# Three transfers for each block of weights, with the first half issued ahead of the store of a converted piece

## The chip, the core and the metric

The kernel runs on one NeuronCore of a Trainium2 chip. The metric is the device time of one execution in microseconds (us), as the median of several runs. The engines are named as in the profile: PE multiplies matrices, ACT (ScalarE), DVE (VectorE) and POOL (GpSimd) work on tiles, and SP issues the transfers between the chip's main memory (DRAM) and the on-chip memory. PE writes its products to the accumulation memory (PSUM), from which ACT and DVE take them.

## What is computed

Attention over a window of 128 keys feeds a mixture of eight experts, and its output feeds a dense two-layer block. Cut to what matters:

```python
def reference(**kwargs):
    attn_out = _attn_ref(q, k, v)                       # 4 x 8 x 576 x 64
    x = attn_out.transpose(0, 2, 1, 3).reshape(2304, 512)
    # mixture of experts: P is softmax(x @ w_gate), normalised 8 times over rows and columns
    for e in range(8):
        h = np.maximum(x @ w1[e], 0.0)                  # 512 -> 1024
        out += P[:, e:e + 1] * (h @ w2[e])              # 1024 -> 512
    # dense block
    h = out @ w_in                                      # 512 -> 2048
    return (np.maximum(0.01 * h, h) @ w_out).astype(np.float32)
```

All inputs are float32 but `w_in` and `w_out` of the dense block, which are float64: 512 x 2048 and 2048 x 512 numbers. [...]

## The kernel before

**Chunks.** The hidden dimension is cut into chunks of 512: 16 chunks of the experts (two for each) and 4 of the dense block, 20 in all. For each chunk the kernel needs a 512 x 512 block of the first weight (`W[0]`) and one of the second (`W[1]`). The tokens are cut into 18 tiles of 128, taken in five pairs of groups (`PAIRS`). For each chunk and pair `a_steps` makes the hidden values (matmuls at L732) and `b_steps` multiplies them by the second weight (matmuls at L849) and adds the result to `acc`. Both use a Strassen-like scheme of seven products of half blocks, and each factor is split into a high and a low float16 part. `merge` interleaves the steps of the one with those of the other.

**A block of weights** (class `Weights`). `load` brings it from DRAM into `raws[0]` or `raws[1]`, tiles of 128 partitions by 4 slots by 512 float32; a slot is 256 KB. There is one such tile for each of the two weights, and it is used again for every chunk. Then `largest` (L580, ACT) squares each of the four slots and sums the squares; `scale_jobs` makes a power of two from the sums (DVE at L413, a small PE matmul at L421, then more DVE work, and a second small matmul at L440); `scaled` (L583, ACT) multiplies each slot by it; `sums` (L607, POOL) and `part` (L446 on ACT, L447 on POOL) make the seven float16 factors.

**A float64 piece** (`to_single`). There are 32 pieces of 128 x 512 numbers. `load` (L655) brings one as 1024 words a partition, which fill slots 0 and 1 of the same raw tile; slot 2 (`fac`) takes sign and exponent, slot 3 (`man`) the mantissa. Five jobs follow: `exponent` (L661 on DVE, L664 on ACT), `signed` (L667, DVE), `high` (L672 on DVE, L673 on ACT), `low` (L679 on ACT, then POOL's addition at L681, the last reader of the words in slots 0 and 1), and `put` (POOL's multiplication at L685 of slot 2 with slot 3 into slot 3, and the store of slot 3 to DRAM at L686). The stored pieces are the weights of the last four chunks.

**Who uses which tile.** `side_jobs` lists the side work of a chunk: up to three pieces, the loads of the next chunk's weights (`a` into `raws[0]`, `b` into `raws[1]`), and their scaling. The first piece lies in `raws[0]`, and `a.load` comes after its `put`; the second and third piece lie in `raws[1]`, and `b.load` comes after the `put` of the third. Ten chunks convert three pieces each, an eleventh two; there `b.load` doesn't follow a third piece.

**Order.** `tick` takes a job from the list after most steps of the matmuls and holds its instructions on ACT, DVE and POOL behind the latest evictions (`anchor`); transfers are not held so. Within these limits and those of the data, a scheduler fixes the order of instructions on each engine at build time, after a simulated timeline (`schedule_with_timeline_sim=True` at the end of the file). On the chip each engine runs its instructions in that order and stands where one has to wait. All transfers are issued by SP, in its order. A transfer into a slot has to wait until the last reader or writer of that slot is done.

In the load before, the first transfer covers slots 0 to 2 and so waits for the multiplication (it reads slot 2); the second covers slot 3 and waits for the store to land.

Of the kernel before, what the change touches and what calls it, by code (L numbers as in the profile page):

```python
# [31 lines left out]
def attn_moe_kernel(  # L32
# [12 lines left out]
    nc = tc.nc  # L45
    P = 128
# [5 lines left out]
    KT = DM // P  # L52
# [496 lines left out]
    chunks = []  # L549
# [14 lines left out]
    class Weights:  # L564
# [5 lines left out]
            self.mx = small.tile([P, 4], F32, tag="mxw", name="mxw")  # L570

        def load(self):
            self.raw = raws[self.which]
            src = chunks[self.ci][self.which].rearrange("(k p) f -> p k f", p=P)
            for ks in (slice(0, KT - 1), slice(KT - 1, KT)):
                nc.sync.dma_start(self.raw[:, ks], src[:, ks])

        def largest(self, k):
            junk = stg.tile([P, FC], BF16, tag="junk", bufs=1, name="junk")
# [55 lines left out]
    def weights(ci):  # L635
        for which in range(2):
            W[which][ci] = Weights(ci, which)

    def to_single(n, place):
# [48 lines left out]
        def words_f32(w):  # L688
            return w.bitcast(F32)

        return load, [exponent, signed, high, low, put]


# [307 lines left out]

    cast = list(range(2 * KT * (F2 // FC)))

    def side_jobs(ci, n):

        todo = [to_single(cast.pop(0), place) for place in range(min(n, len(cast)))]
        weights(ci)
        a, b = W[0][ci], W[1][ci]
        jobs = [load for load, _ in todo[:2]]
        if not todo:  # L1010
            return [a.load, b.load] + [None] * 10 + a.scale() + a.early() + b.scale() + b.early()
        jobs += [None] * 8 + todo[0][1] + [a.load]
        if len(todo) > 1:
            jobs += todo[1][1]
        if len(todo) > 2:
            jobs += [todo[2][0]] + [None] * 4 + a.scale() + todo[2][1] + [b.load] + a.early()
        else:
            jobs += [b.load] + [None] * 8 + a.scale() + a.early()
        return jobs + [None] * 8 + b.scale() + b.early()
# [15 lines left out]
    for n, u in enumerate(units + [None]):  # L1035
        a, b = [], b_steps(*prev)
        if u == LAST:
            held_back = b[7:]
            b = b[:7]
        if u is None:  # L1040
            b = held_back[:3] + [f for two in zip(b, held_back[3:] + [None] * 3) for f in two if f is not None]
        if u is not None:
            ci, p = u
            assert ci < NCE or p in split_pairs
            a = a_steps(ci, p)
            k0 = len(a) - 7
            if p == ends[ci] and ci + 1 < NC:
                a = [[f] + ([lambda j=k - k0: W[0][ci + 1].at(j)] if k >= k0 else []) for k, f in enumerate(a)]
            else:
                a = [[f] for f in a]  # L1050
        if prev[1] == ends[prev[0]] and prev[0] + 1 < NC:
            k0 = len(b) - 7
            b = [[f] + ([lambda j=k - k0: W[1][prev[0] + 1].at(j)] if k >= k0 else []) for k, f in enumerate(b)]
        else:
            b = [[f] for f in b]
        if u is not None and ci >= 1:
            if n and units[n - 1][0] != ci and ci != NCE:
                weigh(ci)
            if p == 4:
                side += side_jobs(ci + 1, 3 if ci < NCE - 1 else 0) if ci + 1 < NC else []  # L1060
# [65 lines left out]
```

## Time and profile before

| | |
|---|---|
| time, median of 3 runs | 1917.11 us (1916.19 to 1918.63) |
| profiled execution: time, span | 1914.87 us, 1913.1 us |
| PE busy | 1848.6 us (97%), 17725 matmuls |
| ACT, DVE, POOL busy | 71%, 69%, 69% |
| loads of expert weights | 32 of 768 KB (median 4.8 us to landing), 32 of 256 KB (3.7 us) |
| loads of float64 pieces | 32 of 512 KB (3.7 and 3.4 us) |
| stores of pieces | 32 of 256 KB (3.3 and 2.2 us) |

The span is the time from the first to the last instruction of the profiled execution, and its own time lies 1.8 us above it. An engine's busy time counts its instructions; where a matmul row is a little longer than its spacing, rows overlap. A row of a timeline gives the start, the duration, the engine, the line in the kernel, the operation, and in brackets how long the engine stood idle before it and what ended that. The attention fills the first 200 us or so, the chunks that convert float64 pieces run from 290 to about 1160 us, then come three loads of expert weights without pieces, and the four chunks of the dense block.

### The profile page before, as it was taken

The page shows a single profiled execution, that of the slowest core. Times are in us where ns is not written, and L with a number is a line of the kernel's source. Part 1 is how long each engine was busy: PE and PEld are TensorE (multiplying, and loading weights), DVE is VectorE, ACT ScalarE, POOL GpSimd, SP SyncE. Part 2 cuts the span into 40 slices and gives each one's busy share as a digit, 9 for nine tenths or more (in the row PEclk, how much of TensorE's full clock was granted, in tenths as well). Part 3 has the DMA queues.
Part 4 walks back from the last instruction along what each step waited for, and adds up shares of the span by engine and source line. Part 5 has one row for each costly group of instructions (what it writes and reads, how often), then busy time and mean ns, then how long its engine had stood idle before and what let it go on. Part 6 is the DMA issues. An engine that isn't in the chain of part 4 may idle for free. (4 is left out here: it accounts for less than half of the span.)

```text
span 1913.1 us, 45183 instructions
## 1 busy us (share of the span) xinstructions
PE 1848.6 (97%) x17725; PEld 1608.6 (84%) x17725; DVE 1317.9 (69%) x3608; ACT 1358.0 (71%) x3123; POOL 1324.6 (69%) x1140
## 2 busy tenths in 40 slices
PE   7899889999999999999999999999999998999999
PEld 5677778888888888988888898988889787889888
DVE  5456567767776777777676767666666687677877
ACT  7978767776767767676776667666675779776754
POOL 3843567777868787876868786685867786666753
PEclk8999999999999999999999999999999999999999
DMA  7522002111111202111121201100001010101002
GB/s 232 172 89 84 2 23 72 46 62 56 40 57 40 84 24 73 53 54 57 40 64 37 79 23 57 45 24 23 24 24 45 1 45 2 36 11 45 2 26 75
DMA packets 61093, 97.80 MB, mean 51 GB/s; under 512 B 4560, under 2 KB 27600, under 8 KB 60880
## 3 DMA queue, kind: packets, MB, share of 16 engines
q1 hardware_dynamic: 60880, 94.93, 15.5%
q8 instruction: 138, 2.26, 0.5%
q14 instruction: 75, 0.61, 0.1%
HBM read 81.81 MB, written 13.11 MB: 50 GB/s over the span
## 5 line engine op out<-in xcount | busy, mean ns | idle before, releaser
L849 PE MATMUL t<-w,h 128*128 128x256 f16 x7560 | 973.3, 273 | 21.8 <-DVE acc L862 10.4
L732 PEld LDWEIGHTS <-w 128*128 128x128 f16 x8400 | 757.2, 98 | 100.3 <-issue 19.2
L849 PEld LDWEIGHTS <-h 128*128 128x128 f16 x7560 | 730.2, 98 | 119.9 <-issue 33.1
L732 PE MATMUL s<-xp,w 128*128 128x256 f16 (+1 forms) x4872 | 610.4, 262 | 10.2 <-ACT q L756 4.5
L862 DVE SCALAR_TENSOR_TENSOR acc<-t,pu,acc 128x256 f32<-128x256 f32 x866 | 407.5, 477 | 203.7 <-PE t L849 158.8
L805 POOL TENSOR_TENSOR h<-s,h 128x1024 f16<-128x1024 f32 x180 | 387.5, 2153 | 132.7 <-ACT h L802 94.6
L732 PE MATMUL sq<-xp,w 128*128 128x256 f16 (+1 forms) x3528 | 448.4, 262 | 3.3 <-DVE s L761 2.9
L860 POOL TENSOR_TENSOR acc<-acc,part 128x256 f32<-128x256 f32 x322 | 234.9, 732 | 270.0 <-ACT part L859 234.9
L447 POOL TENSOR_TENSOR w<-raw,w 128x512 f16<-128x512 f32 x240 | 277.5, 1166 | 43.5 <-ACT w L446 43.3
L761 DVE SCALAR_TENSOR_TENSOR h<-sq,h 128x512 f16<-128x512 f32 (+1 forms) x352 | 192.2, 551 | 75.5 <-ACT h L780 41.4
L859 ACT ACTIVATE part<-t,pu 128x256 f32<-128x256 f32 x322 | 151.6, 471 | 103.5 <-PE t L849 95.5
L802 ACT ACTIVATE h<-s 128x1024 f16<-128x1024 f32 x180 | 189.6, 1053 | 45.6 <-DVE s L761 43.6
L744 ACT ACTIVATE q<-s 128x256 f32<-128x256 f32 x364 | 137.4, 379 | 74.2 <-PE s L732 57.6
L748 DVE SCALAR_TENSOR_TENSOR sq<-sq,q 128x256 f32<-128x256 f32 x352 | 149.2, 425 | 56.1 <-PE sq L732 48.9
L446 ACT ACTIVATE w<-raw 128x512 f16<-128x512 f32 x240 | 147.8, 628 | 7.9 <-PE t L849 5.9
L780 ACT ACTIVATE h<-sq 128x512 f16<-128x512 f32 x176 | 104.2, 592 | 62.4 <-PE t L849 30.7
L761 DVE SCALAR_TENSOR_TENSOR s<-sq,s 128x256 f32<-128x256 f32 x352 | 145.4, 413 | 1.7
L761 DVE SCALAR_TENSOR_TENSOR s<-sq,q 128x256 f32<-128x256 f32 x352 | 131.6, 414 | 16.4 <-ACT q L756 14.3
L748 DVE SCALAR_TENSOR_TENSOR sq<-s,q 128x256 f32<-128x256 f32 x176 | 75.3, 428 | 85.7 <-ACT q L744 80.3
L580 ACT ACTIVATE junk<-raw 128x512 bf16<-128x512 f32 x160 | 100.1, 626 | 29.2 <-DMA raw<-in_moe_w_dram 27.5
L786 ACT ACTIVATE h<-sq 128x256 f16<-128x256 f32 x176 | 66.7, 379 | 74.5 <-DVE sq L748 64.7
L583 ACT ACTIVATE raw<-raw,sr 128x512 f32<-128x512 f32 x160 | 102.4, 715 | 3.4 <-DVE sr L441 2.9
(142 smaller groups left out, 1717.9 us busy)
## 6 DMA issues: line engine op xcount, KB each, us to landing
raw<-in_moe_w_dram SPq DMA_DIRECT2D x32, 768.0 KB, 4.8
k_t<-in_k_dram SPq DMA_DIRECT2D x16, 512.0 KB, 4.0
raw<-in_moe_w_dram SPq DMA_DIRECT2D x32, 256.0 KB, 3.7
raw<-in_moe_w_in_dram SPq DMA_DIRECT2D x16, 512.0 KB, 3.7
raw<-in_moe_w_out_dram SPq DMA_DIRECT2D x16, 512.0 KB, 3.4
q_t<-in_q_dram SPq DMA_DIRECT2D x18, 256.0 KB, 4.3
v_t<-in_v_dram SPq DMA_DIRECT2D x18, 256.0 KB, 2.7
acc<-in_v_dram SPq DMA_DIRECT2D x18, 256.0 KB, 5.8
```

The costliest lines, as they stand in the source:

```text
L446: nc.scalar.activation(out=hi, in_=src, func=AF.Copy)
L447: return nc.gpsimd.tensor_tensor(out=lo, in0=src, in1=hi, op=ALU.subtract)
L732: nc.tensor.matmul(d[b][:, f, :], t[:, wp, kk, ft * P:(ft + 1) * P], XP[p][:, o, kk, xp, :], start=(i == 0 and f == 0 and j in FIRST), sto ...
L744: nc.scalar.activation(out=q[:, k], in_=ps, func=AF.Copy, scale=CS)
L748: nc.vector.scalar_tensor_tensor(out=block(k), in0=ps, scalar=CS, in1=q[:, k], op0=ALU.mult, op1=ALU.add)
L761: nc.vector.scalar_tensor_tensor(out=out, in0=in0, scalar=sc, in1=in1, op0=op0, op1=op)
L802: nc.scalar.activation(out=h[:, 3:7, 0, :], in_=d["s"], func=AF.Copy)
L805: nc.gpsimd.tensor_tensor(out=h[:, 3:7, 1, :], in0=d["s"], in1=h[:, 3:7, 0, :], op=ALU.subtract)
L849: nc.tensor.matmul(ps, h[:, o, hp, f, tt * P:(tt + 1) * P], w[:, wp, ft, :], start=(i == 0 and j in FIRST), stop=(i == 5), skip_group_chec ...
L859: nc.scalar.activation(out=part, in_=ps, func=AF.Copy, scale=s)
L860: nc.gpsimd.tensor_tensor(out=dst, in0=dst, in1=part, op=ALU.add)
L862: nc.vector.scalar_tensor_tensor(out=dst, in0=ps, scalar=s, in1=dst, op0=ALU.mult, op1=ALU.add)
```

## The change

`load` is cut in two. `load_first` brings slots 0 and 1 in one transfer of 512 KB, `load_rest` slots 2 and 3 in a transfer of 256 KB each. Where a load comes right after the `put` of a piece in the same tile, `over` makes `load_first` part of the job of that `put`, ahead of it, and `load_rest` the job after it. The number of jobs in the list stays the same. All other loads call both parts in a row.

```diff
         def load(self):
+            self.load_first()
+            self.load_rest()
+
+        def transfer(self, ks):
+            src = chunks[self.ci][self.which].rearrange("(k p) f -> p k f", p=P)
+            nc.sync.dma_start(self.raw[:, ks], src[:, ks])
+
+        def load_first(self):
             self.raw = raws[self.which]
-            src = chunks[self.ci][self.which].rearrange("(k p) f -> p k f", p=P)
-            for ks in (slice(0, KT - 1), slice(KT - 1, KT)):
-                nc.sync.dma_start(self.raw[:, ks], src[:, ks])
+            self.transfer(slice(0, 2))
+
+        def load_rest(self):
+            for k in range(2, KT):
+                self.transfer(slice(k, k + 1))
...
+    def over(convert, w):
+
+        def ahead():
+            w.load_first()
+            convert[-1]()
+
+        return convert[:-1] + [ahead, w.load_rest]
+
     def side_jobs(ci, n):
...
-        jobs += [None] * 8 + todo[0][1] + [a.load]
+        jobs += [None] * 8 + over(todo[0][1], a)
...
-            jobs += [todo[2][0]] + [None] * 4 + a.scale() + todo[2][1] + [b.load] + a.early()
+            jobs += [todo[2][0]] + [None] * 4 + a.scale() + over(todo[2][1], b) + a.early()
```

## Rows read from the trace of the kernel before

**Rows 1.** Busy time by stretch: stretch, length, engines (instructions), granted clock, DMA share, GB/s.
```profile
290.00:1165.00 875.00, 859.52 (x8172) 759.95 (x8170) 626.91 (x1573) 615.05 (x1334) 666.98 (x559) 1.00 0.17 55
1201.60:1451.20 249.60, 249.60 (x2398) 222.78 (x2397) 162.03 (x434) 162.98 (x360) 175.58 (x151) 1.00 0.08 27
```

**Rows 2.** Waits, whole span: who waited for whom, us in total, times, longest.
```profile
ACT junk L580 <- DMA raw<-in_moe_w_dram: 27.5, 20, 3.9
```

**Rows 3.** Timeline of ACT: first squares after a pause, and one fourth square.
```profile
322.21 0.63 ACT L580 ACTIVATE junk<-raw 128x512 bf16<-128x512 f32 x1 [1.76 <-DMA raw<-in_moe_w_dram]
...
383.87 0.63 ACT L580 ACTIVATE junk<-raw 128x512 bf16<-128x512 f32 x1 [1.27 <-DMA raw<-in_moe_w_dram]
...
555.41 0.63 ACT L580 ACTIVATE junk<-raw 128x512 bf16<-128x512 f32 x1 [1.57 <-DMA raw<-in_moe_w_dram]
...
725.54 0.63 ACT L580 ACTIVATE junk<-raw 128x512 bf16<-128x512 f32 x1 [1.62 <-DMA raw<-in_moe_w_dram]
...
810.46 0.63 ACT L580 ACTIVATE junk<-raw 128x512 bf16<-128x512 f32 x1 [1.19 <-DMA raw<-in_moe_w_dram]
...
896.31 0.63 ACT L580 ACTIVATE junk<-raw 128x512 bf16<-128x512 f32 x1 [2.04 <-DMA raw<-in_moe_w_dram]
...
899.14 0.61 ACT L580 ACTIVATE junk<-raw 128x512 bf16<-128x512 f32 x1
...
1154.80 0.63 ACT L580 ACTIVATE junk<-raw 128x512 bf16<-128x512 f32 x1 [1.16 <-DMA raw<-in_moe_w_dram]
```

**Rows 4.** Timeline of ACT: exponent of the first piece, three groups.
```profile
712.79 0.71 ACT L664 ACTIVATE raw<-raw,shift 128x512 int32<-128x512 int32 x1
...
798.14 0.71 ACT L664 ACTIVATE raw<-raw,shift 128x512 int32<-128x512 int32 x1
...
883.13 0.71 ACT L664 ACTIVATE raw<-raw,shift 128x512 int32<-128x512 int32 x1
```

**Rows 5.** Timeline of PE: small matmul of the scale, the same three groups.
```profile
737.84 0.22 PE L421 MATMUL mt<-identb,e 128*1 128x128 bf16 x1
...
822.83 0.22 PE L421 MATMUL mt<-identb,e 128*1 128x128 bf16 x1
...
908.60 0.22 PE L421 MATMUL mt<-identb,e 128*1 128x128 bf16 x1
```

**Rows 6.** Timeline of SP at 890 us: issues; the second row merges two.
```profile
890.47 0.33 SPq L686 DMA_DIRECT2D wout<-raw  x1
890.90 2.10 SPq L576 DMA_DIRECT2D raw<-in_moe_w_dram  x2
```

**Rows 7.** Timeline of POOL at 888 us: addition and multiplication of the first piece.
```profile
887.72 1.37 POOL L681 TENSOR_TENSOR raw<-raw 128x512 f32<-128x512 f32 x1 [1.11 <-ACT raw L673]
889.17 1.28 POOL L685 TENSOR_TENSOR raw<-raw 128x512 f32<-128x512 f32 x1
```

**Rows 8.** DMA issues of 889 to 896.4 us: KB each, us to landing.
```profile
raw<-in_moe_w_dram SPq DMA_DIRECT2D x1, 768.0 KB, 5.4
wout<-raw SPq DMA_DIRECT2D x1, 256.0 KB, 2.2
raw<-in_moe_w_dram SPq DMA_DIRECT2D x1, 256.0 KB, 4.3
```

**Rows 9.** Timeline of PE: first matmuls after idle time, behind pauses of ACT.
```profile
330.08 0.81 PE L732 MATMUL s<-xp,w 128*128 128x256 f16 x6 [0.62 <-ACT q L756]
...
387.76 0.81 PE L849 MATMUL t<-w,h 128*128 128x256 f16 x6 [1.18 <-DVE e L415]
...
560.83 1.47 PE L849 MATMUL t<-w,h 128*128 128x256 f16 x12 [0.42 <-DVE acc L862]
...
1156.11 0.81 PE L732 MATMUL s<-xp,w 128*128 128x256 f16 x6 [0.70 <-ACT q L756]
1157.35 0.81 PE L849 MATMUL t<-w,h 128*128 128x256 f16 x6 [0.42 <-DVE acc L862]
```

**Rows 10.** Timeline of DVE at 387 us: the sum of squares.
```profile
387.16 0.16 DVE L413 TENSOR_REDUCE m<-mxw 128x1 f32<-128x4 f32 x1 [2.95 <-ACT junk L580]
```

## The prediction

> **What bounds the kernel now.** I read the busy time of two stretches first [rows 1]. From 290 to 1165 us, where the float64 weights are converted beside the matmuls, PE is busy 859.52 of 875.00 us: 15.48 us are idle. From 1201.6 to 1451.2, where nothing is left to convert, PE is busy all of 249.60 us. So the matmuls are the bound, and a change of the loads can give back at most the idle time of the stretch that converts (and what the start holds). The granted clock is 1.00 of full speed in both, the upper of the two levels (2.4 GHz), so the clock is no part of the case.
>
> Then the waits [rows 2]: ACT stands 27.5 us in 20 pauses before the squares of L580 (the job `largest`), waiting for a weight that is still on its way. One pause of 3.9 us is in the start; the other 19 (23.6 us together) are in the stretch that converts, about two to a group of weights. [rows 3] shows seven of them: 1.16 to 2.04 us each, always before the first of the four squares.
>
> What a pause is worth is read from PE, not from ACT. From some 630 us on the groups run in the same order, so two marks can be compared between groups: the first exponent of the first piece (L664) [rows 4] and PE's small matmul of the scale (L421) [rows 5], with one pause between them. Group at 798: 822.83 - 798.14 = 24.69 us, pause 1.19. Group at 712: 25.05 us, pause 1.62. Group at 883: 25.47 us, pause 2.04. So from 1.19 to 1.62 the group grows by 0.36 for 0.43 us of pause, and from there by 0.42 for 0.42. **A pause of up to some 1.2 us is covered by PE's backlog; what is beyond costs PE its full length.**
>
> **The change part by part.** *Three transfers for two.* Every load is now 512, 256 and 256 KB instead of 768 and 256. That is one more issue of about 0.33 us on SP per load [rows 6]. In the stretch that converts SP stands most of the time waiting for POOL, so it costs nothing there; what would be late next if the cover were gone is the load of the third piece, which stands behind the last transfer on SP. In the start the two loads stand in a row of other loads; two more issues could hold those back by 0.7 us, against which the first half lands earlier than 768 KB do. I take 0 there, with bounds of +0.7 (the two issues) and -3.9 (the whole pause).
>
> *The first half moves ahead of the multiplication and the store.* It overwrites only the words of the piece (slots 0 and 1), so it waits for POOL's addition (L681), no longer for the multiplication (L685). At 883 the addition ends at 887.72 + 1.37 = 889.09, the multiplication at 889.17 + 1.28 = 890.45 [rows 7]; the 768 KB went out at 890.90 [rows 6]. The first half goes out at about 889.1, 1.8 us earlier. Its 512 KB are not in the trace as a weight load; by the rows beside it, it lands after 2.2 us (256 KB) to 5.4 us (768 KB beside a store) [rows 8]: between 891.3 and 894.5, and I take the middle, 892.9. ACT was ready at 896.31 - 2.04 = 894.27 [rows 3]. So the pause goes, or 0.2 us of it stays. The wait that is added: SP now stands at the first half until the addition is done, with the store behind it; the store itself waits for the multiplication that comes later on the same engine, so nobody is held up by that.
>
> *Third quarter.* It still waits for the multiplication and goes out behind the store, where the 768 KB did (890.90). Even with the 4.3 us that 256 KB took behind a large transfer [rows 8] it lands at 895.2; its square is the third, and without the pause two squares of 0.63 us [rows 3] stand before it from 894.27, so it is wanted at 895.5 at the earliest. No cost.
>
> *Last quarter.* It waits for the store to land, as before. Before: out at 890.90 + 2.10 - 0.33 = 892.67 [rows 6], landed 4.3 us later at 896.97 [rows 8], used at 899.14 [rows 3]: 2.17 us to spare, of which the removed pause takes 2.04 in this group and about 1.2 in the usual one. The store now starts with 512 KB in flight ahead of it. If it lands no later, the last quarter is in time, and it no longer shares the engines with 768 KB. If the store takes 4.3 us instead of 2.2 (the row of a 256 KB transfer behind a large one), the last quarter is 2.1 us later: the bounds are 0 and 2.1, and I take under 1, since the first half has a lead of 1.4 us on the store and the last quarter then has the engines to itself. The Trainium skill ("DMA: Bandwidth & Descriptors", section "Queues, rings and completion order") says that each DMA engine takes the descriptors of a ring in their order, by which the store would stand behind what is left of the first half. The 4.3 us of 256 KB behind 768 agree with that; by the rule alone the end at 2.1 would be the nearer one, and it is the third rival below.
>
> *The sum.* Gain where a pause shows on PE. Same-order groups: 0.36 + 0.78 = 1.14 (from the marks above; the pauses near 1.2 count nothing). The other groups differ in order, so I take the idle rows of PE in the wake of a pause [rows 9]. After 383.87: 1.18 us, and here the way is seen: DVE stands 2.95 us at L413 for the last square [rows 10], PE behind DVE. After 555.41: 0.42. After 1154.80: 0.70 + 0.42 = 1.12. After 322.21: 0.62 eight us later, counted half, 0.31. Sum 1.14 + 1.18 + 0.42 + 1.12 + 0.31 = 4.17 us. The profiled execution has a span of 1913.1 and a time of 1914.87 us, 2.2 under the median of the three runs (1917.11); I take the gain off the median: **1917.11 - 4.2 = 1912.9**. Lower bound of the gain: if the cover of 1.2 us holds in the other groups too, only what is beyond it comes back: 0.07 + 0.37 + 0.56 + 1.14 = 2.1 us. Upper bound: 15.48 us, all of PE's idle time in the stretch; half of that is as far as I would go, since PE also idles in groups whose pause is under 1.2.
>
> **The rivals.**
> *The pause only moves, or the cover takes it (no change).* The instructions of ACT and DVE stand in an order that was fixed at build time by a simulated timeline. A pause of about 1 us at nearly every load speaks for squares that were placed where the simulated load had landed. With an earlier first half they may be placed earlier, ahead of evictions, and ACT stands as long as now; or the gaps of PE in [rows 9] are filled with other waits (10 of the 15.48 us lie in no wake that I counted). Against it: the pause depends on the multiplication and the store, which the first half no longer waits for. Gain 0 to 3.8, 1913.3 to 1917; with all of it moved 1917.
>
> *The change does nothing.* If the first half doesn't go out before the multiplication, because an earlier instruction on SP holds it, the time is 1917 as now. SP's rows [rows 6] show nothing issued in that place; small.
>
> *The last quarter comes late (slower).* Store behind the first half, 2.1 us later; of that 0.1 to 1.0 us is spare once the pause is gone, so ACT stands 1.1 to 2.0 us at the fourth square and DVE behind it at L413. Beyond the cover of 1.2 that costs up to 0.8 us a load; at all 11 first loads of a group 8.8 us, less little that the earlier squares give back: 1921 to 1926, say 1923. It decides from the point where the store lands some 1.7 us later than now. That DVE does stop there, and that PE follows, is seen at 387 [rows 9, 10]. The Trainium skill ("DMA: Bandwidth & Descriptors", section "Rules for kernel authors") advises to join small transfers into large ones, which speaks against three for two; here the transfers overlap (768 KB and the store were in flight together), so the extra one is not added whole to the path.
>
> **How the numbers follow.** About 0.2% (3.8 us) is what a measurement of this kernel can tell from no change: 1913.3 to 1920.9. My forecast, gain over 3.8 us: 0.50. Pause moved or covered: 0.30. Change without effect: 0.08. Late last quarter, or an order of the instructions that comes out worse by as much: 0.12. So faster 0.50, same 0.38, slower 0.12. The range reaches down to 1907, a gain of 10 (PE's idle time of the stretch less a third), and up to 1919.5, which takes in no change with its spread and leaves out most of the slower case.
>
> **What would show it.** In the profile after: the waits of L580 for a weight fall from 27.5 us to under 8, of which some 3 in the start; the first half's issue stands on SP before the store; PE's idle time between the same places falls from 15.5 to about 11; L664 to L421 is near 24.7 us in every group, as in the group at 798. Wrong would be: pauses of the same sum at the third or fourth square (moved), or DVE waits at L413 above the present ones with the store's landing well over 2.2 us (late last quarter), or a gain with the pauses still there (then the order of instructions did it).

## The result and the profile after

The changed kernel takes 1928.04 us (median of 5 runs, 1923.58 to 1929.90) against 1918.63 us of the kernel before beside it: a ratio of **1.0051** (95% interval 1.0040 to 1.0062). It is slower by half a per cent, where 1912.9 us were forecast. The profiled execution took 1923.58 us (span 1921.8) against 1914.87 (span 1913.1).

In the rows of after, lines behind the change stand 10 lower than in the kernel before, and those of the loads 2: the squares of L580 are L590, the exponent L664 is L674, `high` L673 is L683, POOL's addition L681 is L691, the load L576 is L578.

Busy time by stretch, the two stretches of [rows 1] (columns as there):

```profile
290.00:1165.00 875.00, 855.27 (x8117) 754.33 (x8115) 617.17 (x1560) 608.77 (x1328) 663.52 (x557) 1.00 0.17 54
1201.60:1451.20 249.60, 248.68 (x2386) 221.51 (x2385) 162.41 (x429) 164.21 (x360) 175.32 (x150) 1.00 0.08 25
```

PE does 8117 matmuls in the first stretch, where it did 8172. At 855.27 / 8117 = 0.105 us each, the 55 that are missing are 5.8 us of work that comes later: two thirds of the 8.7 us by which the two spans differ (both traces hold 17725 matmuls in all, so the counts can be compared). The count of matmuls says more here than the busy time, of which 4.25 us are missing. Most of the loss is in the stretch that converts, where the change is; the rest comes behind it. The granted clock is at its upper level (2.4 GHz) in both stretches, as before.

The waits of ACT and of DVE for transfers, whole span (who waited for whom, us in total, times, longest):

```profile
ACT junk L590 <- DMA raw<-in_moe_w_dram: 32.2, 21, 2.5
...
DVE raw L671 <- DMA raw<-in_moe_w_out_dram: 5.2, 4, 1.5
DVE raw L671 <- DMA raw<-in_moe_w_in_dram: 5.0, 4, 1.6
```

and DVE's in the kernel before:

```profile
DVE raw L661 <- DMA raw<-in_moe_w_in_dram: 3.0, 2, 2.8
```

The pauses that were to go are still there, and their sum has grown: 32.2 us against the 27.5 of [rows 2]. A second wait has grown beside them: DVE now waits 10.2 us in 8 places for the words of a float64 piece, where the kernel before waited 3.0 us in 2.

How this comes about is seen in the group at 720 us. SP first: the first half goes out at 721.05, ahead of the store.

```profile
721.05 0.38 SPq L578 DMA_DIRECT2D raw<-in_moe_w_dram  x1
722.40 0.33 SPq L696 DMA_DIRECT2D win<-raw  x1
722.78 3.40 SPq L578 DMA_DIRECT2D raw<-in_moe_w_dram  x2
730.06 0.33 SPq L665 DMA_DIRECT2D raw<-in_moe_w_out_dram  x1
```

The change does what it says: POOL's addition of the first piece ends at 719.65 + 1.37 = 721.02 and the load follows at once. The rows of POOL, with the second piece's addition at 728.75:

```profile
719.65 1.37 POOL L691 TENSOR_TENSOR raw<-raw 128x512 f32<-128x512 f32 x1 [1.11 <-ACT raw L683]
...
726.65 2.13 POOL L815 TENSOR_TENSOR h<-s,h 128x1024 f16<-128x1024 f32 x1 [3.59 <-ACT h L812]
728.75 1.29 POOL L691 TENSOR_TENSOR raw<-raw 128x512 f32<-128x512 f32 x1
```

The first half's landing, from the DMA issues of 720 to 732 us (KB each, us from issue to landing):

```profile
raw<-in_moe_w_dram SPq DMA_DIRECT2D x1, 512.0 KB, 3.5
```

ACT's timeline of the same group:

```profile
722.64 0.39 ACT L754 ACTIVATE q<-s 128x256 f32<-128x256 f32 x1
724.64 0.63 ACT L590 ACTIVATE junk<-raw 128x512 bf16<-128x512 f32 x1 [1.61 <-DMA raw<-in_moe_w_dram]
...
725.53 1.04 ACT L812 ACTIVATE h<-s 128x1024 f16<-128x1024 f32 x1
...
727.09 0.71 ACT L683 ACTIVATE raw<-raw,ones 128x512 f32<-128x512 int32 x1
```

and of the kernel before, at the same place (the first square there is the one at 725.54 in [rows 3]):

```profile
721.71 1.06 ACT L802 ACTIVATE h<-s 128x1024 f16<-128x1024 f32 x1 [0.47 <-DVE s L761]
722.67 0.36 ACT L744 ACTIVATE q<-s 128x256 f32<-128x256 f32 x1
722.94 0.71 ACT L673 ACTIVATE raw<-raw,ones 128x512 f32<-128x512 int32 x1
```

In the kernel before, ACT wrote the float16 hidden values `h` (L802) and did `high` of the second piece (L673) **ahead** of the first square and then stood still. In the changed kernel the first square stands ahead of both (L812, L683), and ACT asks for the first half at 723.03, 1.98 us after its issue, when it takes 3.5 us to land. So ACT stands as long as before, but now with `h` and `high` behind the pause: `high` runs 12.02 us after the group's first exponent (at 715.07), where it ran 10.15 us after it (at 712.79, [rows 4]). The way from there to PE is in the chain of work of 724 to 737 us:

```profile
726.65 2.13 POOL h L815
728.78 1.26 POOL raw L691
730.05 0.02 issue
730.06 3.39 DMA raw<-in_moe_w_out_dram
733.45 0.03 issue
733.48 0.02 DVEq L671
733.50 0.05 issue
733.55 0.43 DVE raw L671
733.98 1.00 DVE s L771 x3
```

and in the rows of DVE and PE, one each:

```profile
733.55 0.43 DVE L671 TENSOR_SCALAR raw<-raw 128x512 int32<-128x512 int32 x1 [1.25 <-DMA raw<-in_moe_w_out_dram]
...
735.02 1.47 PE L742 MATMUL sq<-xp,w 128*128 128x256 f16 x12 [0.91 <-DVE s L771]
```

`h` and `high` are late, so POOL's addition of the second piece is late (728.75; in this group it comes behind POOL's own step on `h`, which stood 3.59 us for ACT's `h`, while `high` was done at 727.80). So the third piece, which overwrites that piece's words, is loaded late (730.06), so DVE stands 1.25 us at its first operation on those words, with the evictions of the matmul behind it, and PE stands 0.91 us for one of these.

The group before it shows the same: DVE stands 1.57 us at 648.11, and PE 0.86 us at 648.93. The two chunks from 627.65 to 800.21 us (first exponent to first exponent) take 172.56 us with 1609 matmuls; in the kernel before, 627.81 to 798.14 takes 170.33 us with 1610. PE's idle time grows in them from 2.0 to 3.7 us, and the two stops behind late words are 1.77 us of it.

### The profile page after: what moved, and what is told of

Read it like the earlier page. It is cut to its first block, busy times and chain, and to the rows that moved or that the text cites. A ratio compares the mean times of both kernels' runs of the same rounds, so it can differ in the third digit from the quotient of the medians.

```text
span 1921.8 us, 45285 instructions
## 1 busy us (share of the span) xinstructions
PE 1850.3 (96%) x17725; PEld 1607.8 (84%) x17725; DVE 1315.5 (68%) x3608; ACT 1357.7 (71%) x3123; POOL 1325.0 (69%) x1140
## 3 DMA queue, kind: packets, MB, share of 16 engines
q1 hardware_dynamic: 61520, 94.93, 15.6%
## 4 chain that ended last, share of the span: by engine, by line
PE 72%; ACT 9%; DVE 6%; POOL 5%; issue 4%; DMA 4%; SPq 0%; POOLq 0%; DVEq 0%; ACTq 0%
PE t L859 34%; PE s L742 20%; PE sq L742 14%; DMA raw<-in_moe_w_dram 2%; POOL h L815 1%; DVE s L771 1%; ACT e L261 1%; PE o L305 1%; DVE raw L682 1%; DVE h L771 1%; PE pt L288 1%; PE s L249 1%; ACT junk L590 1%; DVE acc L872 1%; POOL xp L447 1%
## 5 line engine op out<-in xcount | busy, mean ns | idle before, releaser
L812 ACT ACTIVATE h<-s 128x1024 f16<-128x1024 f32 x180 | 189.7, 1054 | 40.3 <-DVE s L771 36.9
L590 ACT ACTIVATE junk<-raw 128x512 bf16<-128x512 f32 x160 | 100.3, 627 | 33.0 <-DMA raw<-in_moe_w_dram 32.2
```

The lines of the kernel that those rows point to most:

```text
L812: nc.scalar.activation(out=h[:, 3:7, 0, :], in_=d["s"], func=AF.Copy)
```

## The experiments

"First weight" and "second weight" are the two weights that a group loads over converted pieces (`a` and `b` in `side_jobs`). All ratios are to the kernel before, timed on the same chip, with the 95% interval.

### One part of the change at a time

Three transfers, all behind the store:

```
+        def load():
+            with tc.issue_after(stores[-1].ins):
+                w.load()
...
-        return convert[:-1] + [ahead, w.load_rest]
...
+        return convert + [load]
```

> The loads come in three transfers as in the changed kernel, but all three stand behind the store of the piece on SP; nothing goes ahead of it. On ACT the squares then stand where they stand in the kernel before, behind the `high` of the second piece. Order theory (the loss comes from squares that the schedule puts earlier on ACT because it expects the first half earlier): 1915 to 1920, the time of before (1918.6), since the order on ACT is that of before; third piece's words loaded as early as before. Transfer theory (the third transfer itself costs: issues, more fixed cost of a transfer, last quarter later): 1925 to 1929, the time of the changed kernel (1928.0).

Measured: **1.0003** (0.9995 to 1.0012). The third transfer by itself shows no cost here, although ACT's pauses of the stretch grow from 23.6 to 36.4 us; with a hold (below) it shows 0.2%. The Trainium skill ("DMA: Bandwidth & Descriptors", section "Rules for kernel authors") advises to join small transfers; here the extra one costs between nothing and 0.2%.

Only the first weight's first half ahead, the second weight behind its store in the same way:

```
+    def behind_store(w):
+        with tc.issue_after(stores[-1].ins):
+            w.load()
...
-            jobs += [todo[2][0]] + [None] * 4 + a.scale() + over(todo[2][1], b) + a.early()
+            jobs += [todo[2][0]] + [None] * 4 + a.scale() + todo[2][1] + [lambda: behind_store(b)] + a.early()
```

> Three transfers; the first half goes ahead of the store only for the first weight (behind the first piece), the second weight's three transfers stand behind the store of the third piece. On ACT the first weight's squares stand ahead of `high` of the second piece, the second weight's squares as before. Order theory: most of the loss is here, since `high` releases the addition and that the load of the third piece: 1923 to 1928, with a wait of DVE for the third piece's words in about every second group. Transfer theory: about half of the loss, 1922 to 1924.

Only the second weight's first half ahead:

```
...
-        jobs += [None] * 8 + over(todo[0][1], a)
+        jobs += [None] * 8 + todo[0][1] + [lambda: behind_store(a)]
```

> Three transfers; the first half goes ahead of the store only for the second weight (behind the third piece); the first weight's transfers stand behind the store. The first weight's squares stand on ACT as before. Order theory: little of the loss, 1917 to 1922, since no conversion stands behind the second weight's squares; the pauses there grow to 2.2 to 2.5 us as in the changed kernel, of which PE's backlog covers some. Transfer theory: the other half, 1922 to 1924.

Measured: 1.0011 (1.0002 to 1.0020) and 1.0034 (1.0022 to 1.0046): 1919.2 and 1924.2 us. Both expectations of the order theory were missed (the second result lies 0.2 us above the range of its rival); I had put nearly the whole loss on the first weight. In the kernel with the second weight alone DVE waits only 1.2 us for words and ACT's pauses in the stretch are only 12.5 us, and it is slower all the same. So the late words are not the whole loss, and the sum of ACT's pauses alone foretells nothing.

### The order on ACT

The late `high`, in the kernel before with its two old transfers. For that the first weight's first square moves up in the list of jobs, ahead of `high`, so `high`, `low`, `put` and the third piece's load come one job later:

```
+            exponent, signed, high, low, put = todo[1][1]
...
+            def late_high():
+                with tc.issue_after(a.first.ins):
+                    high()
...
-            jobs += todo[1][1]
...
+            scale = a.scale()
+            jobs += [exponent, signed, scale[0], late_high, low, put]
```

> The kernel before with its two transfers; only the `high` of the second piece (first weight's place) is put behind the first square on ACT, as in the changed kernel. If the order of the square and `high` is what costs there: the addition comes later, the third piece's words are loaded later, DVE waits for them at the exponent as at 733 in the changed kernel, PE loses about 1 us in some groups: 1919 to 1925. If `high` has slack: 1915 to 1919.

Measured: **1.0056** (1.0043 to 1.0069), 1928.1 us, more than the 1919 to 1925 that I expected, and as much as the whole change loses (1.0051), with no transfer changed. (That the two are so near is in part chance: the runs below show more than one effect in the 1.0051.) Its waits, whole span, and ACT's rows at 731 us:

```profile
DVE raw L662 <- DMA raw<-in_moe_w_in_dram: 4.8, 5, 1.3
DVE raw L662 <- DMA raw<-in_moe_w_out_dram: 4.8, 5, 1.5
```
```profile
730.43 0.63 ACT L580 ACTIVATE junk<-raw 128x512 bf16<-128x512 f32 x1 [1.81 <-DMA raw<-in_moe_w_dram]
...
731.07 0.70 ACT L674 ACTIVATE raw<-raw,ones 128x512 f32<-128x512 int32 x1
```

It is the same picture: a pause of 1.81 us, `high` behind it, POOL's addition at 731.85 after 1.82 us of waiting for `high` (here `h` stands ahead of the pause, at 726.76), and DVE waiting for the third piece's words, in ten places.

The other way round, the changed kernel with only this order put back, so that the first weight's first square comes behind `high`:

```
+    def after_high(jobs):
+        def first():
+            with tc.issue_after(highs[-1].ins):
+                jobs[0]()
+        return [first] + jobs[1:]
...
-            jobs += [todo[2][0]] + [None] * 4 + a.scale() + over(todo[2][1], b) + a.early()
+            jobs += [todo[2][0]] + [None] * 4 + after_high(a.scale()) + over(todo[2][1], b) + a.early()
```

> The changed kernel with one thing held: on ScalarE the first square of the first weight comes behind `high` of the second piece, as in the kernel before. The first square of the second weight stays as early as in the changed kernel, right behind the four `scaled` activations. Theory (the loss is the order of ScalarE, and both places have a part in it): the third piece's words come in time again, DVE's waits for words fall from 10.7 us to under 2, and the time falls from 1928 to 1918 to 1925, near that of the kernel in which only the second weight's first half goes ahead (1924). Rival A (only the late `high` costs): 1905 to 1912, as in the kernel whose two first squares wait for the second transfer. Rival B (the late `high` costs nothing here): 1926 to 1930.

Measured: 1905.35 us, **0.9940** (0.9924 to 0.9955), and a second time, beside other kernels:

> The changed kernel with `high` of the second piece ahead of the first weight's first square, a second time, beside the three others: 1902 to 1909, or a ratio of 0.992 to 0.996, if its first result stands; over 1912 if that was chance.

1904.61 us, 0.9942 (0.9928 to 0.9956). My own theory (1918 to 1925) was wrong here and rival A right: the order at the first weight turns a loss of 0.5% into a gain of 0.6%. Its rows: busy time of the stretch; the waits for transfers, whole span; SP and ACT at 882 us:

```profile
290.00:1165.00 875.00, 868.38 (x8283) 770.69 (x8281) 632.01 (x1598) 634.06 (x1358) 671.87 (x565) 1.00 0.18 55
```
```profile
ACT junk L590 <- DMA raw<-in_moe_w_dram: 10.4, 12, 2.7
...
DVE raw L673 <- DMA raw<-in_moe_w_out_dram: 0.6, 2, 0.3
DVE raw L673 <- DMA raw<-in_moe_w_in_dram: 0.5, 2, 0.3
```
```profile
882.47 0.38 SPq L578 DMA_DIRECT2D raw<-in_moe_w_dram  x1
883.82 0.33 SPq L698 DMA_DIRECT2D wout<-raw  x1
```
```profile
886.52 0.72 ACT L685 ACTIVATE raw<-raw,ones 128x512 f32<-128x512 int32 x1
887.15 0.61 ACT L590 ACTIVATE junk<-raw 128x512 bf16<-128x512 f32 x1
```

The first half has 4.68 us from its issue to its square, and ACT doesn't stop for it. The pauses are 10.4 us (27.5 before, 32.2 in the changed kernel), DVE's waits for words 1.1 (3.0 and 10.2), and PE does 8283 matmuls in the stretch, 111 more than before: at 0.105 us, 11.7 us, of which 1.7 are work that the start left over (2625 against 2641 up to 290 us). The two profiled spans differ by 9.3 us, the medians by 1917.13 - 1905.35 = 11.8.

### The holds

Here the first square also waits for the third quarter, so the schedule can't place it early, at both weights (run twice), at the first alone (`self.which == 0`) and at the second alone:

```
...
-            nc.scalar.activation(out=junk, in_=self.raw[:, k], func=AF.Square, accum_out=self.mx[:, k:k + 1])
+            ins = nc.scalar.activation(out=junk, in_=self.raw[:, k], func=AF.Square, accum_out=self.mx[:, k:k + 1])
+            if k == 0:
+                behind(ins, self.last[2])
```

> All transfers as in the changed kernel, the first half ahead of the store, but the first square of each load also waits for the transfer of slot 2, so the schedule puts the squares back behind where they stood before. Order theory: 1912 to 1919, at or under the time of before; the pauses of ACT at the first square shrink from 32 us to 15 to 25, and PE's waits for the third piece (0.9 us a group) are gone. Store theory (the first half in flight ahead of the store makes the store and so the last quarter late): the store lands well over 2.2 us, DVE waits at the sum of the squares more than now, 1923 to 1929.

> The changed kernel with the first square of each weight waiting for the third slot's transfer too, a second time, beside the kernels with one hold each: 1906 to 1911, or a ratio of 0.993 to 0.997, if its first result stands; over 1914 if that was chance.

> The changed kernel; only the first weight's first square also waits for the transfer of the third slot. The second weight's squares stay as early as in the changed kernel. Theory (both places have a part): 1917 to 1924. Rival A (the gain of the kernel with both holds is of the first weight alone): 1906 to 1911. Rival B (it is of the second alone): 1926 to 1930.

> The changed kernel; only the second weight's first square also waits for the transfer of the third slot; the first weight's first square stands ahead of `high` of the second piece in some of the chunks, as in the changed kernel. Theory (both places have a part): 1913 to 1922, with more of DVE's waits for words than the 1.1 us of the kernel with both holds. Rival A (the gain is of the first weight alone): 1926 to 1930. Rival B (it is of the second weight alone, whose squares no longer stand right behind the four `scaled` activations): 1906 to 1911.

Measured: both weights 0.9952 (0.9939 to 0.9965) and 0.9957 (0.9945 to 0.9969), the first alone 0.9957 (0.9945 to 0.9969), the second alone 1.0006 (0.9997 to 1.0015). For the first alone rival A is right (1909.1 us), for the second alone the theory (1918.5 us). The first result for both weights, 1908.3 us, lies below the range of the order theory (1912 to 1919). Holding the first weight's square is enough for the gain of both; holding the second's alone takes the loss away without a gain.

The same hold without the change (the kernel before, waiting for its second transfer; then three transfers behind the store, waiting for the third quarter), and a hold for the last quarter in the changed kernel:

> The transfers of the kernel before (768 and 256 KB, both behind the store), but the first square of each load also waits for the second transfer, so that the schedule puts all four squares later on ACT. Order theory (what counts is where the squares stand on ACT; the transfers themselves are worth nothing): 1906 to 1912, most of the gain that the changed transfers with held squares gave (1908.3 against 1916.9). Theory that the first half ahead of the store is what gains once the order is right: 1915 to 1920.

> Three transfers, all behind the store, and the first square waits for slot 2; on ACT the squares stand exactly where they stand in the kernel before, so this differs from it by the transfers alone. Order theory: 1914 to 1919, the time of before (1916.9). Transfer theory (a third transfer costs by itself): 1920 or more.

> The transfers of the changed kernel, the first square of each load waits for the last quarter, so the squares stand still later on ACT than with the wait for slot 2. Order theory: pauses of ACT before squares fall under 15 us, 1904 to 1911. Theory that an early chain of the scale matters (squares, sum, small matmul): later squares cost, 1912 to 1918.

Measured: 0.9992 (0.9984 to 1.0001), 1.0017 (1.0009 to 1.0026) and 1.0042 (1.0030 to 1.0055). The first is where it was expected if only the first half ahead gains. The second, 1920.4 us, missed the order theory (1914 to 1919) and lies in the range of the transfer theory: with the squares where the kernel before has them, three transfers show a cost of 0.2%. The hold by itself gains nothing; of the kernels here it gains only with a first half that goes out ahead. Held as far as the last quarter it loses nearly as much as the change, outside both expectations: there is no wait for words left, but ACT's pauses in the stretch are 36.7 us. That miss is what showed me that both have to be right, the order and the time of landing.

### The second weight, and each weight with its order in place

`high` ahead of the first square as above, together with (1) only the first weight's half ahead, (2) the hold of the second weight's square; and (3) only the second weight's half ahead, with that hold:

> Only the first weight's first half goes ahead of the store (the second weight's three transfers are all held behind theirs), and the first weight's first square is held behind `high` of the second piece. Differs from the kernel in which only the first weight goes ahead (1.0011) by that hold alone. Theory (a late `high` is the cost, and the transfers gain at the first weight's place once it is in time): 1904 to 1912, or a ratio of 0.993 to 0.997. Rival A (the gain needs the second weight's first half ahead too): 1914 to 1919. Rival B (the late `high` is not what costs here): 1918 to 1922.

> The changed kernel with `high` of the second piece ahead of the first weight's first square (0.994 alone) and also the second weight's first square held for the third slot's transfer. Theory A (early squares of the second weight cost): 1896 to 1904. Theory B (they cost nothing): 1904 to 1909.

> Only the second weight's first half goes ahead of the store, and its first square waits for the third slot's transfer too, so that ScalarE's order there is again that of the kernel before. Differs from the kernel in which only the second weight goes ahead (1.0034) by that hold alone. Theory A (there it was the early squares of the second weight that cost): 1908 to 1917. Theory B (it was something else, such as the first weight's three transfers behind the store, whose pauses stay): 1920 to 1926.

Measured: (1) 1923.2 us, 1.0029 (1.0016 to 1.0041), outside all three expectations; (2) 1900.54 us, **0.9915** (0.9901 to 0.9928), and (3) 1908.58 us, 0.9959 (0.9946 to 0.9971), both as theory A has it. The hold of the second weight's square is worth 1.0034 - 0.9959 = 0.75% where only that weight goes ahead, 0.25% beside `high` in time, 0.45% in the changed kernel (1.0051 to 1.0006), and nothing beside the hold of the first weight (0.9957 alone, 0.9952 and 0.9957 with both). So early squares of the second weight cost too, in three of four pairs. Version (2) beats both kernels. Its busy time in the stretch:

```profile
290.00:1165.00 875.00, 871.77 (x8323) 774.84 (x8321) 638.34 (x1602) 633.70 (x1364) 677.66 (x569) 1.00 0.18 55
```

PE does 151 more matmuls than before, 15.8 us; the profiled spans differ by 16.5 us, the medians by 17.0.

The kernels whose squares stand on ACT as in the kernel before, or later (behind `high` at the first weight, at least three places behind the last `scaled` at the second), sorted by ACT's pauses of 290 to 1165 us:

| first half ahead | squares held by | pauses, us | ratio |
|---|---|---|---|
| both weights | `high` / third quarter | 10.2 | 0.9915 |
| second weight | third quarter | 15.6 | 0.9959 |
| first weight | `high` / - | 20.6 | 1.0029 |
| none, two transfers | second transfer | 22.5 | 0.9992 |
| none (the kernel before) | - | 23.6 | 1 |
| none, three transfers | third quarter | 29.2 | 1.0017 |
| none, three transfers | - | 36.4 | 1.0003 |
| both weights | last quarter | 36.7 | 1.0042 |

With the order in place, fewer pauses go with less time, roughly: between the last two rows and the first, some 26 us of pauses go with 0.9 to 1.3%, 17 to 24 us. The rows differ in more than their pauses, so this is a likeness and no proof. (With both holds the square is one place ahead of `high` in five of ten groups: 19.8 us of pauses, 0.9952.) Where the order is not in place, the kernel is slower than this list has it: the changed kernel (29.8 us, 1.0051), the late `high` (32.6 us, 1.0056), the second weight alone without the hold (12.5 us, 1.0034). The third row doesn't fit. Its trace shows one thing that the pauses leave out: DVE waits 6.4 us in nine places for the words of pieces, nearly as in the kernel with only the first weight ahead (8.4 us in seven), though `high` stands ahead of the square. What makes the words late there was not followed. The last two rows differ by 0.4% with the same pauses. Both stay open (below).

## Why the prediction was wrong

**What held.** The first half goes out ahead of the store, right behind POOL's addition, and lands 3.5 us later (taken: 3.8, the middle of 2.2 and 5.4). The third transfer costs little (1.0003, and 1.0017 beside the hold). The bound is PE, and the change acts in the stretch that converts.

**The step that failed** is "So the pause goes, or 0.2 us of it stays", with ACT ready at 894.27. It moved the landing and left ACT's order as it was. The order of the instructions is made anew for the changed kernel, and the squares moved up ahead of `h` and `high`, to a place that suits a landing after some 2 us, not 3.5. In the group at 712, whose pause was 1.62 us, it is 1.61 us in the changed kernel, and from the first exponent (715.07) to the small matmul (740.14) it takes 25.07 us, against the 25.05 of [rows 4, 5]: no gain at all there. Every second group is longer: those at 627, 800 and 972 take 26.8 to 27.3 us, where they took 24.7 (part of this is work, 250 matmuls between the marks at 627 against 238). The pauses don't fall under 8 us but rise to 32.2.

**The rival "the pause only moves"** had this mechanism ("they may be placed earlier, ahead of evictions, and ACT stands as long as now") and was priced at a gain of 0 to 3.8 us. The price was wrong: I asked only how long ACT stands, not what stands behind it. What moved behind the pause were the steps on which POOL's addition and the next piece's load wait, and with the old transfers a late `high` cost 0.56% without any gain beside it (1.0056). The slower cases had 0.12, one of them "an order of the instructions that comes out worse by as much", without a mechanism or a place; it should have had both, since the pauses of [rows 3] already showed squares placed ahead of their data.

**The rival "the last quarter comes late"** is not what happened. There is a trace of it: the store at 894.92, the one that answers to [rows 8] and now stands behind 512 KB, takes 3.3 us where it took 2.2. The Trainium skill ("DMA: Bandwidth & Descriptors", section "Queues, rings and completion order") says that an engine takes a ring's descriptors in order, and this number agrees with it; the other half of the stores, those of `w_in`, don't show it (3.0 us in the median, 3.3 before). In the group at 811 the fourth square waits 0.92 us, for another reason (last section), but DVE's wait at L413 in the stretch falls from 11.5 to 7.0 us, and the kernel with `high` in time has the same transfers and is fast.

**The sum was too small.** With the order in place the mechanism of the forecast works: the pauses fall from 27.5 to 10.4 us and the time by 11.8 us, where the sum gave 4.2. The term that was mis-sized is the price of a pause: "A pause of up to some 1.2 us is covered by PE's backlog" came from three groups of one kernel, none with a pause under 1.19 us: they show what more pause costs beyond that, and nothing of a cover below it. A chunk without a pause shows it. In the kernel with `high` in time, the chunk from 707.92 to 791.57 us has none before a square, and PE is busy all of its 83.65 us, with 805 matmuls. In the kernel before, the chunk from 798.14 to 883.13, with pauses of 1.19 and 0.88 us, takes 84.99 us for the same 805 matmuls. So pauses that counted nothing in the sum go with 1.34 us a chunk. The list above, where some 26 us of pauses go with 17 to 24 us of time, points the same way: most of a pause is not covered. The upper bound was too low as well: PE's idle time of 15.48 us. An undisturbed stretch shows why: in the kernel with `high` in time, PE is busy all of 810 to 980 us and does 1630 matmuls, 0.1043 us each. At that rate 875 us hold 8390 matmuls; the kernel before did 8172, which is 218 or 22.7 us short (an estimate from these counts). The busy time hides stops too short to be listed: a matmul takes 0.1052 us of it in the kernel before (859.52 / 8172), 0.1043 here. So the range (1907 to 1919.5) missed the measured time and would have missed the fast version too. Its lower end, a gain of 10 us, also lies beyond "half of that is as far as I would go", which is 7.7 us.

**What stays open.** Why only the first weight's half ahead, with `high` in time, is slower (1.0029) than none ahead (1.0003), with late words again, while it gains 0.44% where the second weight's half is ahead too (0.9959 to 0.9915); whether the third transfer costs nothing or 0.2%; and why a hold for the last quarter costs 0.4% over kernels with the same pauses. Nor is the way traced by which early squares of the second weight reach PE; the runs show only that they cost. Each edit makes ACT's, DVE's and PE's order anew in more places than the one that was held, so a pair of kernels never differs in one instruction alone.

## What to carry to other kernels

Where the order of an engine is made from planned times, an earlier transfer can move its readers up too, here further than the transfer really gained; what then stands behind the waiting reader has a large part in the price, not only the length of the wait. So read which instructions follow the reader on its in-order engine and who waits for them, and hold the reader where it was (by an explicit order behind the step that others need) when a load is moved forward: here that made +0.5% into -0.6%, and with the second reader held too -0.85%. Count the matmuls of a stretch against the rate of an undisturbed one; busy time alone understates what can be won.

## What the runs showed of the hardware

One thing was not expected: the fetch of program code holds back transfers of data. In the kernel with only the first weight's half ahead and `high` in time, the DMA engines nearly stop in the middle of a group while transfers are under way. This is the DMA view of 895 to 907 us, in 40 equal slices (busy share in tenths, then GB/s), and its line on the queue that brings instructions (transfers, MB, share of the time of 16 engines):

```profile
DMA  0000000138999898997200000000000269997998
GB/s 0 0 0 0 0 0 0 48 143 314 375 403 348 314 307 212 246 328 280 102 21 0 0 14 7 20 27 27 14 0 0 48 225 369 307 253 300 382 362 328
...
q8 instruction: 1, 0.02, 0.9%
```

The first half went out at 896.20, the store at 897.61 and the third quarter just behind it. From 897.4 to 900.7 the engines move 140 to 400 GB/s; after a standstill some 7 to 27 GB/s trickle until 903.6, and the third quarter's square starts only at 904.12, after a pause of 1.66 us. The fourth then waits 1.01 us more.

The trace's packets show why. One transfer of instructions, 16384 bytes, starts at 900.23 and takes 1.76 us (0.9% of 16 engines over 12 us is one engine for 1.7 us). At 901.97, as it ends, sixteen packets of 2048 bytes begin to go one behind the other, and from 901.9 to 903.7 the busy share is 6.1%, that of one engine in 16. They are 32 KB, a sixteenth of the store (256 KB) and a sixteenth of the third quarter (256 KB). So one engine, busy with the instructions, had its shares of both still to do when the others were through; the two landed 5.8 and 6.0 us after their issue. The group at 811 of the changed kernel shows it too: a transfer of instructions from 813.38 to 815.17, then eight packets alone up to 816.34, and the fourth square stands 0.92 us until 816.94.

Each execution has 138 such transfers, 63 to 65 of them in the stretch that converts (in the four traces that were counted: before, after, `high` in time, and this one), of 0.9 to 1.9 us each. Only a few of ACT's pauses have one close before them; one ran from 892.34 to 893.41 us during the load before the longest pause of [rows 3] (2.04 us). Whether they have a part in the differences between the kernels is not shown. A schedule that plans a landing from the size of a transfer alone can't foresee them.
